# Query tiles of one attention unit with two buffers, in place of tiles of two units with one buffer

## The chip, the cores and the metric

The kernel runs on one core of a Trainium2 chip. A core has five engines with a queue of instructions each: TensorE (PE, matrix products), VectorE (DVE), ScalarE (ACT), GpSimd (POOL) and SyncE (SP, which here only starts transfers). An engine takes its instructions in the order of its queue; an instruction that waits for another engine or for a transfer holds everything behind it. Transfers are started from the queues of SP and ACT. The metric is the time on the device in microseconds (us), from one launch to its end.

## What is computed

Attention with a top-32 mask over 4 batches, 8 heads, 576 positions and 64 channels, followed by two feed-forward layers of 512 to 2048 to 512 over the 2304 tokens, the first with a rational function, the second with h*cos(h):

```python
scores = scale * np.matmul(q, k.transpose(0, 1, 3, 2))
kth = np.partition(scores, -top_k, axis=-1)[..., -top_k:-top_k + 1]
mask = scores >= kth
scores = np.where(mask, scores, -1000000000.0)
scores = scores - np.max(scores, axis=-1, keepdims=True)
attn = np.exp(scores)
attn = attn / (np.sum(attn, axis=-1, keepdims=True) + 1e-09)
return np.matmul(attn, v).astype(np.float32)
...
h = x @ w_in
g = P / (Q + 1e-06)          # P, Q: polynomials of h and |h|
x = g @ w_out
...
h = x @ w_in
g = h * np.cos(h)
return (g @ w_out).astype(np.float32)
```

All is float32. To keep that precision the kernel splits most operands of its matrix products into a rounded high part (type float32r) and the rest (low part), and adds two or three products.

## The kernel before

**Units and pieces.** Attention is cut into 72 units. A unit is 128 query rows of one pair of heads. Eight units (4 pairs of heads times 2 row tiles) make one block of 256 tokens; there are 9 blocks. Two neighbouring units, an even one and the odd one behind it, share the pair of heads and the block, so their queries lie side by side in memory. The program is written as a list of pieces, five for each unit (p = 0 to 4). In a piece of unit i stand steps of several units: the scores of unit i+1 (`qk`, L328), the top-32 search of unit i (`topk`, L356), the end of the mask and the product with V of unit i-1 (`av`, L405), and steps of the feed-forward layers of earlier blocks (`in1`, `pol1`, `end1`, `low1`, `out1` and their likes of the second layer).

**Scores.** `qk(i)` makes the scores of the two heads j = 0 and 1 in turn. For each it runs four matmuls into one PSUM tile `sx`: high part of q times k (L346) and low part of q times k (L348), for two halves of the keys. ACT then copies `sx` to `sS`. For units 0 to 7 (the first block) the raw q is used without a split (L343). The first half of `qk(i+1)` stands at the head of unit i, the second in its piece p = 0 (for units 20 and up).

**Queries.** `load_q(i)` (L194) fetches the tile `qr`, 128 partitions x 2 x 256 values, 256 KB, the queries of units i and i+1, by a transfer that is started from ACT's queue. It stands in p = 1 of an even unit, two units ahead. `split_q(i)` (L200) has ACT copy `qr` with rounding into `qh` and, one piece later, has DVE (for i from 20 to 71) or POOL (before) subtract `qh` from `qr` into `ql`. It stands in p = 3 and p = 4 of an even unit and serves the two units that follow. `qr`, `qh` and `ql` have one buffer each (`QRB`, `QHB` = 1): a new `qh` can be written only when the last matmul that reads the old one is done, and that is the second half of `qk(i+1)`, where i is the even unit in which the split stands.

**Order.** The order within each queue is made when the kernel is built, by a planned timeline that starts whatever is ready, the earlier written first. Three wrappers add to that. `InOrder` (L91) holds DVE, in units 20 to 71, to the order in which the program is written. `Behind` (L114) makes POOL's instructions there wait for the last instruction of DVE other than MAX8 and MATCH_REPLACE8 that was written before them. `Windowed` (L72) bounds how far an engine may run ahead in the first pieces. In units 20 to 71 the order on DVE is therefore: in p = 0 the feed-forward steps `end1` (u, q, u, u), the mask of the unit before (e), max and min of two halves of the scores (e), `mid2` (rr); then rounds of MAX8 and MATCH_REPLACE8 up to p = 4; then, in even units, the subtraction into `ql`.

**Phases.** Units 0 to 19, up to about 340 us, run beside the conversion of the weights. Units 20 to 71 end at about 1160 us. Behind them stand only feed-forward steps.

Of the kernel before, what the change touches and what calls it, by code (L numbers as in the profile page):

```python
# [23 lines left out]
P = 128  # L24
# [10 lines left out]
BT = 2 * P  # L35
# [22 lines left out]
DGL, E1P, M2P, LAL = 0, 4, (12, 12), 3  # L58
DV1, DV2 = 8, 7
KB, VB, XB = 2, 2, 2  # L60
SQ, OBB, EB = 3, 1, 2
QRB, QHB = 1, 1
LQ = 1
S0, MD, O1P, I2, O2, SB = 46, 4, 1, 2, 3, 4
U0, U1 = 20, 72
C0, C1 = 5 * U0, 5 * U1 - 4
# [64 lines left out]
def body(tc, out, qt, kt, vt, ident_d, w1_d, w1o_d, a_d, b_d, w2_d, w2o_d):  # L131
    nc = tc.nc
    V, A = InOrder(tc, nc.vector, WIN, C0), Windowed(tc, nc.scalar, WA, PA)
    G = Behind(tc, nc.gpsimd, WG, PG, v=V)
    PE, SP = nc.tensor, nc.sync

    with ExitStack() as ctx:
# [6 lines left out]
        att = pool("att", 2)  # L144
# [20 lines left out]
        nu = len(units)  # L165
# [23 lines left out]
            SP.dma_start(out=x[:, 0].bitcast(F32), in_=kt[b, pr])  # L189
            return x  # L190

        qpair, vlast = {}, [None]
# [42 lines left out]

        load_q(0)
        load_k(0)
        ident = cst.tile([P, P], F32)
        SP.dma_start(out=ident, in_=ident_d)
        nident = cst.tile([P, P], F32R)  # L240
# [86 lines left out]

        def qk(i):  # L328
            n, pr = units[i]
            raw, hi, lo = (*qpair[i // 2], None, None)[:3]  # L330
            kvs = ins[i]
            m = P // len(kvs)
            st[i] = sb = att.tile([P, 2, S], F32, tag="sS", bufs=2, name=f"sS{i}")
            for j in range(2):
                rows = slice(j * D, (j + 1) * D)
                for c, (k, _) in reversed(list(enumerate(kvs))):
                    q0 = i % 2 * P
                    qs, qc = slice(0, (c + 1) * m), slice(q0, q0 + (c + 1) * m)
                    for hf in range(2):
                        o = sx[qs, hf, :HALF]  # L340
                        hs = slice(hf * HALF, (hf + 1) * HALF)
                        if n < 2:
                            mm = PE.matmul(o, raw[rows, j, qc], k[rows, 0, hs].bitcast(F32), start=True, stop=True)  # L343
                            after(mm, hf)
                        else:
                            mm = PE.matmul(o, hi[:, j, qc], k[:, j, hs], start=True, stop=False, skip_group_check=True)  # L346
                            after(mm, hf)
                            mm = PE.matmul(o, lo[:, j, qc], k[:, j, hs], start=False, stop=True, skip_group_check=True)  # L348
# [379 lines left out]
        def attention():  # L728
            load_k(1)
            load_v(0)  # L730
            for _ in qk(0):
                pass
            prev = None
            nrm, fresh, held, sq = [], [], [], None
            for i in range(nu + 1):
                if LQ == 0 and i % 2 == 0 and i + 2 < nu:
# [12 lines left out]
                for p in range(5):  # L749
                    if p == 0 and grouped:  # L750
                        yield
                        next(prev)
                        next(prev)
                        next(t)
                    elif p == 0:
                        if prev is not None:
                            next(prev)
                        next(t, None)
                        if prev is not None:
                            next(prev)  # L760
                        next(t, None)
                    else:
                        next(t, None)
                    if p == 0:
                        if prev is not None:
                            a = av(i - 1)
                            next(a)
                        next(nq, None)
                        if prev is not None:
                            next(a, None)  # L770
                            if i % 4 == 0:
                                nrm.append(norm((i - 1) // 8, (i - 1) // 4 % 2))
                                next(nrm[-1])
                                next(nrm[-1])
                                fresh.append(nrm[-1])
                        if 0 < i < nu:
                            load_v(i)
                    if p == LQ > 0 and i % 2 == 0 and i + 2 < nu:
                        load_q(i + 2)
                    if p == SQ and i % 2 == 0 and 8 <= i + 2 < nu:  # L780
                        sq = split_q(i + 2)
                        next(sq, None)
                    if p == SQ + 1 and sq is not None:
                        next(sq, None)
                        sq = None
                    if fresh and p == (4 if grouped else 1):
                        next(fresh.pop())
                    if len(nrm) == 2 and (p == 4 or p == 1 and not grouped):
                        for x in nrm if grouped else nrm[:1] if p == 1 else nrm[1:]:
                            next(x, None)  # L790
                        if p == 4:
                            nrm = []
                    yield
                prev = t
# [61 lines left out]
```

## Time and profile before

| | |
|---|---|
| median of 3 runs | 1379.81 us (1376.72 to 1381.07) |
| the profiled execution, time | 1384.74 us |
| the profiled execution, span from the first to the last instruction | 1383.0 us |
| mean granted TensorE clock, share of full speed | 0.940 |

Most numbers below come from the one profiled execution, which took 4.93 us more than the median. Of its 1384.74 us, 1383.0 us are the span and 1.74 us lie around it. In the rows, a name such as `ql<-qr,qh` gives what an instruction writes and what it reads. Most helper calls are recorded under one line, L81, so the tile names are what tells them apart. A bracket at the end of a line gives how long the engine stood idle before it, and what ended that.

### The profile page before, as it was taken

Reading aid. Unit: us, or ns where it says so; the run is one execution under the profiler, and the core shown is the slowest. Engines: PE = TensorE matmul, PEld = TensorE weight load, DVE = VectorE, ACT = ScalarE, POOL = GpSimd, SP = SyncE. Lnnn points to the kernel's source line nnn. Section 1 sums busy time; section 2 is a strip of 40 time slices with the busy share of each in tenths; the row PEclk is TensorE's granted clock in tenths of the full one; section 3 lists DMA queues with packets and bytes.
Section 4 is the critical chain, followed back from the end, with each engine's and each line's share of the span. In section 5 each row is a group of like instructions: output and inputs, shape, how many; then the busy total and the mean of one; then the engine's idle time right before and its main releaser. Section 6 shows DMA issues by size and latency. Waiting matters only on the chain.

```text
span 1383.0 us, 24902 instructions
## 1 busy us (share of the span) xinstructions
PE 1234.3 (89%) x8944; PEld 1100.5 (80%) x8944; DVE 1184.1 (86%) x2477; ACT 1082.2 (78%) x1886; POOL 599.3 (43%) x439
## 2 busy tenths in 40 slices
PE   5676678666998999999999999999999999999997
PEld 2344566555888999899899989998999989899986
DVE  6989987889999998989999998999898888666533
ACT  6876777775787888888888888888888778697653
POOL 2666445543245554535564363545353534430000
PEclk9856788777999999999999999999999999999999
DMA  7996767693557756666776755665666778567787
GB/s 236 331 308 203 241 190 221 235 320 122 160 178 245 255 196 219 199 218 213 240 252 235 236 199 195 210 215 188 218 210 230 265 257 277 194 214 249 237 273 227
DMA packets 141547, 314.97 MB, mean 228 GB/s; under 512 B 12016, under 2 KB 28528, under 8 KB 141424
## 3 DMA queue, kind: packets, MB, share of 16 engines
q1 hardware_dynamic: 122832, 261.99, 57.3%
q10 hardware_dynamic: 18592, 51.39, 11.0%
q8 instruction: 71, 1.16, 0.3%
q14 instruction: 52, 0.43, 0.1%
HBM read 278.20 MB, written 35.13 MB: 227 GB/s over the span
## 4 chain that ended last, share of the span: by engine, by line
PE 47%; DVE 23%; ACT 12%; DMA 10%; issue 4%; POOL 3%; SPq 0%; ACTq 0%; POOLq 0%; DVEq 0%
DVE e L81 10%; PE o L639 8%; PE h L499 6%; PE h L501 6%; PE h L500 6%; DVE hd L81 4%; DVE u L81 4%; PE y L570 3%; PE y L571 3%; PE sx L439 3%; PE y L569 3%; PE sx L346 2%; DMA w2o<-w2o 2%; ACT r L81 1%; PE sx L348 1%
## 5 line engine op out<-in xcount | busy, mean ns | idle before, releaser
L81 DVE MAX8 hd<-e 128x8 f32<-128x288 f32 (+1 forms) x576 | 320.6, 595 | 0.0
L81 DVE MATCH_REPLACE8 e<-hd,e 128x288 f32<-128x288 f32 (+1 forms) x432 | 230.6, 540 | 0.0
L639 PE MATMUL o<-w2o,gg 128*128 128x512 f32 x864 | 218.0, 396 | 3.1 <-DMA w2o<-w2o 2.5
L639 PEld LDWEIGHTS o<-w2o,gg 128*128 128x128 f32 x864 | 155.6, 189 | 37.7 <-DMA w2o<-w2o 3.8
L570 PE MATMUL y<-gg,w1o 128*128 128x256 f32 x576 | 169.0, 293 | 8.5 <-POOL gg L81 8.5
L499 PE MATMUL h<-xh,w1hi 128*128 128x256 f32 x576 | 170.9, 297 | 5.9 <-ACT pt24a L81 1.6
L569 PE MATMUL y<-gg,w1o 128*128 128x256 f32 x576 | 171.0, 297 | 2.9 <-ACT gg L81 2.9
L81 POOL TENSOR_TENSOR rr<-rr,hs 128x512 f32<-128x512 f32 x56 | 72.7, 1300 | 222.5 <-DVE rr L81 127.2
L571 PE MATMUL y<-gg,w1ol 128*128 128x256 f32 x576 | 167.2, 290 | 1.2 <-DMA w1ol<-w1ol 1.2
L500 PE MATMUL h<-xl,w1hi 128*128 128x256 f32 x576 | 167.1, 290 | 0.0
L501 PE MATMUL h<-xh,lo 128*128 128x256 f32 x576 | 166.4, 289 | 0.5 <-DMA lo<-w1lo 0.5
L501 PE MATMUL h<-x2h,lo 128*128 128x256 f32 x576 | 163.5, 284 | 0.7 <-DMA lo<-w2lo 0.6
L499 PE MATMUL h<-x2h,w2hi 128*128 128x256 f32 x576 | 163.8, 285 | 0.2 <-ACT pt64b L81 0.2
L500 PE MATMUL h<-x2l,w2hi 128*128 128x256 f32 x576 | 163.3, 284 | 0.0
L81 POOL TENSOR_TENSOR gg<-u,gg 128x512 fp32r<-128x512 f32 x64 | 85.2, 1332 | 139.0 <-DVE rr L81 86.8
L81 DVE TENSOR_TENSOR e<-sS 128x576 f32<-128x576 f32 x144 | 125.5, 911 | 16.1 <-PE sx L425 8.8
L81 DVE SCALAR_TENSOR_TENSOR e<-sS,hd,e 128x576 f32<-128x576 f32 x144 | 130.7, 935 | 4.7 <-ACT e L81 4.6
L81 POOL TENSOR_TENSOR cb<-cb,raw 128x512 int32<-128x512 int32 x64 | 91.6, 1433 | 81.6 <-DVE cb L81 73.1
L570 PEld LDWEIGHTS y<-gg,w1o 128*128 128x128 f32 x576 | 114.4, 199 | 12.0 <-POOL gg L81 10.0
L499 PEld LDWEIGHTS h<-xh,w1hi 128*128 128x128 f32 x576 | 114.0, 198 | 10.6 <-ACT pt24a L81 1.8
L569 PEld LDWEIGHTS y<-gg,w1o 128*128 128x128 f32 x576 | 114.1, 198 | 5.7 <-ACT gg L81 3.7
L571 PEld LDWEIGHTS y<-gg,w1ol 128*128 128x128 f32 x576 | 114.3, 198 | 2.6 <-DMA w1ol<-w1ol 1.4
(1028 smaller groups left out, 3656.4 us busy)
## 6 DMA issues: line engine op xcount, KB each, us to landing
w2o<-w2o SPq DMA_DIRECT2D x144, 512.0 KB, 4.4
lo<-w1lo SPq DMA_DIRECT2D x72, 512.0 KB, 3.9
w1ol<-w1ol SPq DMA_DIRECT2D x72, 512.0 KB, 4.3
lo<-w2lo SPq DMA_DIRECT2D x72, 512.0 KB, 4.8
k<-kdr ACTq DMA_DIRECT2D x44, 576.0 KB, 4.8
raw<-w SPq DMA_DIRECT2D x32, 512.0 KB, 5.3
v<-vt ACTq DMA_DIRECT2D x48, 320.0 KB, 5.2
qr<-qt ACTq DMA_DIRECT2D x36, 256.0 KB, 3.8
```

Source lines behind the costliest of these rows:

```text
L81: r = f(*a, **k)
L346: mm = PE.matmul(o, hi[:, j, qc], k[:, j, hs], start=True, stop=False, skip_group_check=True)
L348: mm = PE.matmul(o, lo[:, j, qc], k[:, j, hs], start=False, stop=True, skip_group_check=True)
L439: mm = PE.matmul(o, v[:, kc * P + j * D:kc * P + (j + 1) * D], pj[j][:, kc, qs], start=False, stop=(kc == 3), skip_group_check=True)
L499: PE.matmul(h[:, i, :], wh, xh[:, c, :], start=(c == 0), stop=False)
L500: PE.matmul(h[:, i, :], wh, xl[:, c, :], start=False, stop=False)
L501: PE.matmul(h[:, i, :], lo[:, i, c, :], xh[:, c, :], start=False, stop=(c == NCC - 1))
L569: PE.matmul(y[:, c, :], w1o[:, f, cs], gh[:, i, :], start=(f == 0 and c % 2 == 0), stop=False, skip_group_check=True)
L570: PE.matmul(y[:, c, :], w1o[:, f, cs], gl[:, i, :], start=False, stop=False, skip_group_check=True)
L571: PE.matmul(y[:, c, :], wl[:, i, cs], gh[:, i, :], start=False, stop=(f == NF - 1), skip_group_check=True)
L639: PE.matmul(o[:, t, :], l[:, i, ts], wt[i][:, r], start=(f == 0 and r == 0 and l is gh), stop=(f == NF - 1 and l is gl), skip_group_check= ...
```

## The change

A tile of q now holds one unit: 128 partitions x 2 x 128 values, 128 KB. The raw tile `qr` has two buffers. High and low part lie in one tile `q` of 2 x 2 x 128 values, with two buffers. So 6 KB for each partition hold queries before and after. Each unit has its own fetch, copy and subtraction. In unit i, p = 0 subtracts for unit i+2 (`low_q`; on DVE in units 20 to 71, on POOL before), p = 1 fetches for unit i+4 (for i+3 while the first block runs), and p = 2 copies for unit i+3 (`high_q`). The subtraction stands at the end of what attention does in p = 0, so on DVE it lies between max and min of the scores and `mid2`.

```diff
+QRB, QB = 2, 2
...
         def load_q(i):
-            k, pr = units[i][0] // 2, units[i][1]
-            raw = att.tile([P, 2, BT], F32, tag="qr", bufs=QRB, name=f"qr{i}")
-            A.dma_start(out=raw, in_=qt[k, pr])
-            qpair[i // 2] = (raw,)
-
-        def split_q(i):
-            raw, = qpair[i // 2]
-            hi = att.tile([P, 2, BT], F32R, tag="qh", bufs=QHB, name=f"qh{i}")
-            lo = att.tile([P, 2, BT], F32R, tag="ql", bufs=QHB, name=f"ql{i}")
-            A.activation(hi, raw, AF.Copy)
-            qpair[i // 2] = (raw, hi, lo)
-            if U0 <= i < U1:
-                yield
-                V.tensor_sub(lo, raw, hi.bitcast(F32))
-            else:
-                G.tensor_sub(lo, raw, hi.bitcast(F32))
+            if i < nu:
+                k, pr = units[i][0] // 2, units[i][1]
+                raw = att.tile([P, 2, P], F32, tag="qr", bufs=QRB, name=f"qr{i}")
+                A.dma_start(out=raw, in_=qt[k, pr, :, :, i % 2 * P:(i % 2 + 1) * P])
+                qs_[i] = [raw, None]
+
+        def high_q(i):
+            if 8 <= i < nu:
+                qs_[i][1] = x = att.tile([P, 2, 2, P], F32R, tag="q", bufs=QB, name=f"q{i}")
+                A.activation(x[:, 0], qs_[i][0], AF.Copy)
+
+        def low_q(i, E):
+            if 8 <= i < nu:
+                raw, x = qs_[i]
+                E.tensor_sub(x[:, 1], raw, x[:, 0].bitcast(F32))
...
-                    if p == LQ > 0 and i % 2 == 0 and i + 2 < nu:
-                        load_q(i + 2)
-                    if p == SQ and i % 2 == 0 and 8 <= i + 2 < nu:
-                        sq = split_q(i + 2)
-                        next(sq, None)
-                    if p == SQ + 1 and sq is not None:
-                        next(sq, None)
-                        sq = None
+                    if p == 0:
+                        low_q(i + 2, V if grouped else G)
+                    if p == 1:
+                        if i + 1 < 8:
+                            load_q(i + 3)
+                        if i + 2 >= 8:
+                            load_q(i + 4)
+                    if p == 2:
+                        high_q(i + 3)
```

`grouped` is true in units 20 to 71. The matmuls of `qk` keep their number, shapes and order; they read the unit's own tile.

## Rows read from the trace of the kernel before

**Rows 1.** The page's first part: busy time, share of the span and instructions.
```profile
PE 1234.3 (89%) x8944; PEld 1100.5 (80%) x8944; DVE 1184.1 (86%) x2477; ACT 1082.2 (78%) x1886; POOL 599.3 (43%) x439
```
**Rows 2.** Windows: length, busy PE, PEld, DVE, ACT, POOL (instructions), clock, DMA share, GB/s.
```profile
773.50:900.00 126.50, 122.60 (x963) 115.03 (x962) 117.40 (x259) 107.28 (x187) 59.20 (x45) 0.99 0.63 209
900.00:1026.50 126.50, 122.61 (x962) 115.01 (x962) 117.38 (x259) 107.23 (x187) 59.17 (x45) 0.99 0.63 210
```
**Rows 3.** Waits of DVE, 773.5 to 900 us: us in total, times, longest us.
```profile
DVE ql L81 <- ACT qh L81: 5.8, 2, 3.4
DVE rr L81 <- ACT n L81: 2.4, 1, 2.4
DVE q L81 <- ACT r L81: 0.5, 1, 0.5
```
**Rows 4.** Timeline, 784 to 794 us: start, us, engine, line, operation, tiles, shapes.
```profile
786.12 1.44 ACT L81 ACTIVATE e<-sS,nb 128x576 f32<-128x576 f32 x2
...
786.46 0.29 PE L348 MATMUL sx<-k,ql 128*128 128x288 f32 x1
...
787.45 0.62 ACT L81 ACTIVATE qh<-qr 128x512 fp32r<-128x512 f32 x1
...
788.11 0.69 DVE L81 TENSOR_TENSOR ql<-qr,qh 128x512 fp32r<-128x512 f32 x1 [2.35 <-ACT qh L81]
...
788.72 0.74 DVE L81 SCALAR_TENSOR_TENSOR u<-u,nega,w 128x512 f32<-128x512 f32 x1
788.83 0.34 ACTq L81 DMA_DIRECT2D qr<-qt  x1
...
792.85 1.42 DVE L81 TENSOR_TENSOR e<-sS 128x576 f32<-128x576 f32 x2
```
**Rows 5.** Waits of DVE, then of ACT, 300 to 1100 us.
```profile
DVE ql L81 <- ACT qh L81: 29.6, 12, 3.4
...
ACT qh L81 <- PE sx L346: 8.1, 12, 1.6
```
**Rows 6.** The chain that ended last, 500 to 950 us: start, us, work.
```profile
535.87 0.63 ACT qh L81
...
913.91 0.63 ACT qh L81
```
**Rows 7.** Waits of PE, 773.5 to 900 us.
```profile
PE y L570 <- POOL gg L81: 1.8, 1, 1.8
```
**Rows 8.** Windows behind that wait (columns as in rows 2).
```profile
828.00:833.00 5.00, 5.00 (x30) 5.00 (x31) 5.00 (x14) 4.45 (x9) 4.01 (x4) 0.66 0.02 7
```
**Rows 9.** Groups by line and shape, whole run: busy us, mean ns | idle before.
```profile
L81 DVE MAX8 hd<-e 128x8 f32<-128x576 f32 x288 | 203.7, 745 | 0.0
...
L81 DVE MAX8 hd<-e 128x8 f32<-128x288 f32 x288 | 117.0, 445 | 0.0
...
L81 ACT ACTIVATE qh<-qr 128x512 fp32r<-128x512 f32 x32 | 20.0, 625 | 8.5 <-PE sx L346 8.4
...
L81 DVE TENSOR_TENSOR ql<-qr,qh 128x512 fp32r<-128x512 f32 x26 | 17.8, 684 | 39.5 <-ACT qh L81 39.5
...
L81 POOL TENSOR_TENSOR ql<-qr,qh 128x512 fp32r<-128x512 f32 x6 | 9.3, 1549 | 15.4 <-ACT qh L81 10.5 <-DMA w2o<-ch 4.9
```
**Rows 10.** Timeline of DVE, 816 to 818 us.
```profile
816.59 0.67 DVE L81 TENSOR_TENSOR ql<-qr,qh 128x512 fp32r<-128x512 f32 x1
817.18 0.74 DVE L81 SCALAR_TENSOR_TENSOR u<-u,nega,w 128x512 f32<-128x512 f32 x1
```
**Rows 11.** Instructions on tile qr: its fetch (ns min/median/max), and time to landing.
```profile
L81 ACTq DMA_DIRECT2D qr<-qt x36: 334/335/468, 0.7 to 1107.3; - x36
...
DMA to landing us min/median/max: 2.4/3.8/6.9
```
**Rows 12.** A window behind the last unit (columns as in rows 2).
```profile
1200.00:1250.00 50.00, 49.69 (x401) 47.94 (x402) 26.15 (x35) 37.34 (x57) 15.50 (x12) 1.00 0.61 204
```

More of the change, by code (lines that the diff above doesn't have):

```diff
@@ L60 @@
 KB, VB, XB = 2, 2, 2
-SQ, OBB, EB = 3, 1, 2
-QRB, QHB = 1, 1
-LQ = 1
+OBB, EB = 1, 2
+QRB, QB = 2, 2
 S0, MD, O1P, I2, O2, SB = 46, 4, 1, 2, 3, 4
@@ L190, in prep @@
             return x
-        qpair, vlast = {}, [None]
+        qs_, vlast = {}, [None]
         def load_q(i):
-            k, pr = units[i][0] // 2, units[i][1]
-            raw = att.tile([P, 2, BT], F32, tag="qr", bufs=QRB, name=f"qr{i}")
-            A.dma_start(out=raw, in_=qt[k, pr])
-            qpair[i // 2] = (raw,)
-        def split_q(i):
-            raw, = qpair[i // 2]
-            hi = att.tile([P, 2, BT], F32R, tag="qh", bufs=QHB, name=f"qh{i}")
-            lo = att.tile([P, 2, BT], F32R, tag="ql", bufs=QHB, name=f"ql{i}")
-            A.activation(hi, raw, AF.Copy)
-            qpair[i // 2] = (raw, hi, lo)
-            if U0 <= i < U1:
-                yield
-                V.tensor_sub(lo, raw, hi.bitcast(F32))
-            else:
-                G.tensor_sub(lo, raw, hi.bitcast(F32))
+            if i < nu:
[11 more added lines that the diff above has]
+                E.tensor_sub(x[:, 1], raw, x[:, 0].bitcast(F32))
         def load_k(i):
@@ L237, in body @@
         load_k(0)
+        load_q(1)
         ident = cst.tile([P, P], F32)
@@ L329, in qk @@
             n, pr = units[i]
-            raw, hi, lo = (*qpair[i // 2], None, None)[:3]
+            raw, x = qs_.pop(i)
+            hi, lo = (x[:, 0], x[:, 1]) if x is not None else (None, None)
             kvs = ins[i]
@@ L336, in qk @@
                 for c, (k, _) in reversed(list(enumerate(kvs))):
-                    q0 = i % 2 * P
-                    qs, qc = slice(0, (c + 1) * m), slice(q0, q0 + (c + 1) * m)
+                    qs = slice(0, (c + 1) * m)
                     for hf in range(2):
@@ L342, in qk @@
                         if n < 2:
-                            mm = PE.matmul(o, raw[rows, j, qc], k[rows, 0, hs].bitcast(F32), start=True, stop=True)
+                            mm = PE.matmul(o, raw[rows, j, qs], k[rows, 0, hs].bitcast(F32), start=True, stop=True)
                             after(mm, hf)
                         else:
-                            mm = PE.matmul(o, hi[:, j, qc], k[:, j, hs], start=True, stop=False, skip_group_check=True)
+                            mm = PE.matmul(o, hi[:, j, qs], k[:, j, hs], start=True, stop=False, skip_group_check=True)
                             after(mm, hf)
-                            mm = PE.matmul(o, lo[:, j, qc], k[:, j, hs], start=False, stop=True, skip_group_check=True)
+                            mm = PE.matmul(o, lo[:, j, qs], k[:, j, hs], start=False, stop=True, skip_group_check=True)
                         order[hf] = [mm.ins.name]
@@ L732, in attention @@
                 pass
+            load_q(2)
             prev = None
-            nrm, fresh, held, sq = [], [], [], None
+            nrm, fresh, held = [], [], []
             for i in range(nu + 1):
-                if LQ == 0 and i % 2 == 0 and i + 2 < nu:
-                    load_q(i + 2)
                 nq = qk(i + 1) if i + 1 < nu else iter(())
@@ L777, in attention @@
                             load_v(i)
-                    if p == LQ > 0 and i % 2 == 0 and i + 2 < nu:
-                        load_q(i + 2)
-                    if p == SQ and i % 2 == 0 and 8 <= i + 2 < nu:
-                        sq = split_q(i + 2)
-                        next(sq, None)
-                    if p == SQ + 1 and sq is not None:
-                        next(sq, None)
-                        sq = None
+                    if p == 0:
[7 more added lines that the diff above has]
+                        high_q(i + 3)
                     if fresh and p == (4 if grouped else 1):
```

## The prediction

> **What bounds the kernel now.** I read the busy shares first, then windows of eight units, then who waits for whom, then the chain of work that ended last, and at last the timeline around the one step that the change moves. By the busy shares of the whole run PE leads with 89%, DVE follows with 86% and ACT with 78% [rows 1]. That is an average over three phases, so it decides nothing yet.
>
> Units 20 to 71 repeat every eight units, in about 126.5 us, and two such stretches look alike to within 0.1 us [rows 2]. In the first of them PE is busy 122.60 us, so it idles 3.9; DVE is busy 117.40 and idles 9.1; ACT idles 19.2, which is 2.4 us for each unit. Of DVE's 9.1 us, 5.8 + 2.4 + 0.5 = 8.7 are three waits [rows 3]. DVE takes its instructions in the written order here, so a wait holds all that stands behind it: DVE is working or held in 126.1 of 126.5 us, which makes it the tightest engine, with PE close behind. Its largest wait is the one for `qh`, twice in a stretch.
>
> The timeline shows how that wait comes about [rows 4]. DVE stands 2.35 us before the subtraction into `ql`, until 788.11. It waits for ACT's rounding copy into `qh`, which runs from 787.45. The copy could not start earlier than about 786.7, for the last matmul that reads the old `qh` and `ql` starts at 786.46 and takes 0.29 us, and there is one buffer; by then ACT was in two exponentials (786.12, 1.44 us). Behind the subtraction DVE has the feed-forward steps u, q, u, u, on which POOL and then PE wait.
>
> Between 300 and 1100 us this wait comes 12 times and costs DVE 29.6 us; the copy itself waits for matmuls 12 times, 8.1 us in all [rows 5]. In the chain that ended last the copy stands four times between 500 and 950 us, once for each stretch; the first and the last are shown [rows 6]; the other wait of a stretch is not on it.
>
> Behind the last unit PE is busy 49.69 of 50 us and DVE 26.15 [rows 12]: there nothing that is done to q can shorten anything.
>
> **The change part by part.**
>
> *The copy.* It moves from p = 3 of the unit before its use by two pieces and a unit ahead. With two buffers of one unit it writes over unit i+1 while it stands in unit i, so it still waits for the second half of `qk(i+1)`, the same matmuls as before. What changes is the deadline. Before, DVE wanted the result one piece later; now it wants it in p = 0 of the next unit, behind u, q, u, u, the two masks and max and min. In the timeline the matmul ends near 786.75, and max and min of the next p = 0 end at 794.27 [rows 4]; without the wait and the subtraction ahead of them that would be near 791.3, so ACT has about 4.5 us in which to place a copy of half a microsecond. I take the wait for `qh` as gone: 29.6 us less in DVE's queue at most.
>
> *ACT's work.* 32 copies of 512 values become 64 of 256. A whole copy takes 625 ns [rows 9]; a half one lies between 313 ns and that, so the addition is between 0 and 32 x 0.625 = 20 us over the run. I take 5 us, from the slope of DVE's MAX8 below, as the nearest pair of shapes. It is covered by ACT's idle 2.4 us per unit, of which 5 us over 64 units use 0.08. Without that cover it would cost the 5 us. The copy's own wait for matmuls can come twice as often, which is 16 us in place of 8.1, or 0.2 us a unit, and lies in the same cover.
>
> *DVE's work.* 26 subtractions of 512 values become 50 of 256 (units 22 to 71; units 20 and 21 go to POOL). MAX8 takes 745 ns for 576 values and 445 for 288 [rows 9], so 1.04 ns a value; a half subtraction is then 684 - 267 = 417 ns, and the pair costs 0.15 us more than the whole. In the queue the next instruction starts 0.59 us after the subtraction's start [rows 10], so a half one may take up only 0.32 us and the pair 0.06 us more. Added: 25 x 0.06 to 25 x 0.15 = 1.5 to 3.8 us. I take the upper end, since a result is awaited at its end.
> [...]
>
> *POOL's work.* Before unit 20, 6 subtractions of 1549 ns [rows 9] become 14 halves. A half takes between 0.77 and 1.55 us, so 14 take 10.8 to 21.7 in place of 9.3. POOL is busy 43% [rows 1] and I take nothing for it, with 12 us as the worst, all of it exposed. The two waits named in the same row, 15.4 us, may go with the longer lead, so the other end is as far below nothing.
>
> *Transfers.* 36 fetches become 72, each of half the bytes but in runs of 512 bytes in place of 2 KB. A fetch of 256 KB lands in 3.8 us, at most 6.9 [rows 11]; the new ones are asked for more than a unit, 15.8 us, before the copy. Even at twice the longest they are hidden. Starting one takes 0.335 us in ACT's queue [rows 11], so 36 more are 12 us at most, or 0.25 us a unit, in ACT's cover; in the timeline ACT's engine ran on beside it.
>
> *A wait that is added.* The fetch for unit i+4 goes into the buffer that the subtraction for unit i+2 has just read, and stands one piece behind it. ACT's queue is held until DVE is done with it. Behind it stand the copies of transposed scores, `sS` and the exponentials, on which PE and DVE wait. Such a hold is there already: the fetch was started at 788.83, 0.03 us after the subtraction ended (788.11 + 0.69) [rows 4], and ACT lost next to nothing. It will come in each unit in place of every second. I take nothing for it, as in that row, and price the other end as a rival.
>
> *What is late next.* Without the wait DVE reaches u, q, u, u 2.35 us sooner, so POOL's subtraction `gg` comes sooner too, on which PE stood 1.8 us in this stretch [rows 7]. [...] Then ACT is next: DVE's wait for `n` (2.4 us) and for `r` [rows 3] will grow a little, for ACT is paced by PE's results.
>
> **The sum.** On the chain the wait stands four times: 4 x 2.35 = 9.4 us. The loss of clock goes in the two stretches that show 0.99 [rows 2]: 2 x 1.7 = 3.4. Against that, the chain carries the subtraction in eight places or so: 8 x 0.15 = 1.2. Gain 9.4 + 3.4 - 1.2 = 11.6 us. The profiled execution would go from 1384.7 to 1373.1; it lay 4.9 us above the median of 1379.8, which goes to **1368**. The bounds of the unknown costs (POOL 12 us more, or 15 us less) put this case between 1352 and 1380, the likeliest part being 1360 to 1375.
>
> **The rivals.**
>
> *The whole wait comes out.* All 29.6 us of DVE's wait turn into time, less 1.5 of added work: 28.1, so 1352. For it: DVE is working or held nearly always. Against it: PE has only 3.9 us of idle time in 126.5, and 29.6 us over 6.3 stretches are 4.7 each.
>
> *PE binds and nothing is gained.* If PE's 122.6 us and the waits on ACT that have nothing to do with q set the pace, DVE only waits elsewhere, and the time stays at 1379, between 1376 and 1384. The chain speaks against it, since it runs through DVE from 788 us on.
> [...]
>
> *The wait stays.* ACT's copy still waits for the same matmuls. If the queue's order places it late, DVE waits in p = 0 instead and only the costs are left: 1379.8 + 3.8 = 1384.
>
> *ACT is held by the fetch: slower.* If ACT comes to the fetch when DVE has only begun p = 0, it is held until the subtraction is done, by the timeline about 5.5 us (788.72 to 794.27 [rows 4]), and the exponentials and `sS` of that unit come late. ACT can lose 2.4 us a unit before it sets the pace; from there on each hold counts. Once in eight units, as the order repeats: (5.5 - 2.4) x 6.5 = 20 us, so 1400; once in sixteen, 1390. For it: every unit now has such a fetch, and ACT has long waits on PE and POOL of its own. Against it: the plan places the fetch where the subtraction should be done, and the one hold seen cost nothing.
>
> **How the numbers follow.** Forecast 0.45 (1368); the whole wait 0.12 (1352); PE binds 0.14 (1379); the wait stays 0.07 (1384); ACT held 0.22 (1390 to 1400). The order of every queue is planned anew, which can move the first 340 us either way; that is in the POOL bounds. The range leaves out about one in ten at each end: the lower part of the whole wait, and the dearer half of the held fetch: 1348 to 1392. A measurement of this kernel tells about 0.3% from no change, 1375.7 to 1384.0. Faster takes the forecast and the whole wait, 0.57. Same takes PE binding and most of the staying wait, 0.20. Slower takes the held fetch and the rest, 0.23.
>
> **What would show it.** Right: DVE's wait for the copy below 5 us in all, between 300 and 1100 us; stretches of eight units of about 124.5 us; no mean clock of 0.99 in them; ACT's idle time before instructions that follow a fetch as now. Wrong: a wait of DVE for ACT's copy in p = 0; fetches that start right behind the subtraction with ACT idle for over a microsecond before them; or DVE waiting for `n`, `r` or the exponentials by as much as it had waited for `qh`.

## The result: slower by 0.9%, and what the profile shows

The changed kernel takes 1391.56 us (median of 4 runs, 1390.32 to 1395.74) against 1380.44 beside it: 1.0091 times the time before, with an interval of 1.0063 to 1.0120. The forecast was 1368, so even the sign is wrong; the time lies at the foot of the rival "ACT is held by the fetch". The profiled execution took 1395.74 us, 1393.9 of them span.

The busy shares of the page hardly differ from [rows 1]:
```profile
PE 1245.6 (89%) x8944; PEld 1104.1 (79%) x8944; DVE 1172.3 (84%) x2501; ACT 1084.9 (78%) x1918; POOL 584.2 (42%) x447
```
Where the time went shows in the timeline of DVE, at max and min of the scores of unit 20 and of unit 71 (two of these instructions a unit, so units can be counted). Before:
```profile
366.74 1.42 DVE L81 TENSOR_TENSOR e<-sS 128x576 f32<-128x576 f32 x2
...
1181.94 1.43 DVE L81 TENSOR_TENSOR e<-sS 128x576 f32<-128x576 f32 x2 [0.38 <-ACT sS L81]
```
After:
```profile
350.21 1.42 DVE L80 TENSOR_TENSOR e<-sS 128x576 f32<-128x576 f32 x2
...
1193.96 1.43 DVE L80 TENSOR_TENSOR e<-sS 128x576 f32<-128x576 f32 x2 [0.57 <-ACT sS L80]
```
So the whole is a sum of two large changes of opposite sign: the first 20 units end 16.5 us sooner, and units 20 to 71, where the gain was forecast, take 843.8 us in place of 815.2, 28.6 more. The rest behind unit 71 is 1 us shorter. (The section on the kernel before puts the ends of its phases at about 340 and 1160 us; by this count they lie at 367 and 1182.)

DVE's waits between 300 and 1100 us, to be read beside [rows 5] and [rows 3] (total, times, longest):
```profile
DVE e L80 <- ACT sS L80: 42.2, 21, 3.8
DVE q L80 <- ACT r L80: 13.4, 10, 2.2
DVE rr L80 <- ACT n L80: 11.4, 12, 2.2
```
The wait for the rounding copy, 29.6 us before, is gone, as the prediction said. In its place DVE waits 42.2 us for the scores `sS`. The window of one repeat of the schedule (eight units, columns as in [rows 2]) is 128.0 us long in place of 126.5:
```profile
770.90:898.90 128.00, 122.10 (x960) 113.38 (x960) 116.42 (x262) 107.12 (x192) 57.38 (x44) 1.00 0.63 204
```
PE's 122 us of work are the same as in [rows 2]; its idle time went from 3.9 to 5.9 us. This repeat is a mild one. From max to max, units 48 to 55 take 1.5 us more than before, units 40 to 47 take 6.6 more, and from the max of unit 64 to that of unit 71 it is 11.7. The windows of the whole stretch, before and then after:
```profile
366.74:1181.94 815.20, 787.49 (x6250) 736.62 (x6251) 758.37 (x1647) 684.83 (x1191) 392.11 (x289) 0.99 0.67 223
```
```profile
350.21:1193.96 843.75, 798.04 (x6251) 740.56 (x6250) 751.35 (x1673) 687.78 (x1215) 377.41 (x289) 0.99 0.66 215
```
PE idles 45.7 us in place of 27.7, and the same number of matmuls keeps it busy 10.6 us longer. Part of that is the clock. In windows of half a microsecond over these two stretches it reads 1.00 or 0.50, and a value between only where it changes. With a wait of PE of 2.54 us, up to 1104.70, it falls from 1.00 to 0.50:
```profile
1105.00:1110.00 5.00, 5.00 (x24) 4.93 (x24) 4.78 (x10) 0.65 (x1) 3.17 (x3) 0.50 0.39 146
```
PE's busy time in these half microseconds, times the share of the clock that is missing, gives an estimate of what the low clock cost: 5.1 us before and 10.6 after, so about 5.5 us of the longer busy time.

The timeline from 784 to 801 us shows one repeat from near by:
```profile
784.87 0.30 PE L347 MATMUL sx<-k,q 128*128 128x288 f32 x1
...
785.20 0.65 ACT L80 ACTIVATE sS<-sx 128x576 f32<-128x576 f32 x1
...
785.75 0.41 ACT L80 ACTIVATE q<-qr 128x256 fp32r<-128x256 f32 x1
...
785.89 1.43 DVE L80 TENSOR_TENSOR e<-sS 128x576 f32<-128x576 f32 x2 [1.20 <-ACT sS L80]
...
787.23 0.42 DVE L80 TENSOR_TENSOR q<-qr,q 128x256 fp32r<-128x256 f32 x1
...
787.68 0.56 ACTq L80 DMA_DIRECT2D qr<-qt  x1
...
787.83 0.27 PE L438 MATMUL sx<-pt45b,v 128*64 128x128 f32 x1
...
788.29 0.28 ACT L80 ACTIVATE xs<-sx 128x128 f32<-128x128 f32 x1 [2.13 <-DVE rr L80]
...
788.62 0.40 PE L345 MATMUL sx<-k,q 128*128 128x288 f32 x1 [0.52 <-ACT xs L80]
...
794.99 0.27 PE L424 MATMUL sx<-ident,e 128*128 128x128 f32 x1
...
800.60 0.29 PE L345 MATMUL sx<-k,q 128*128 128x288 f32 x1
```
Two things are to be seen. The fetch of the next q starts 0.03 us after DVE's subtraction (787.23 + 0.42), for it goes into the buffer that the subtraction has read, and ACT's engine stands 2.13 us until the copy `xs` behind it. That is not all the fetch's doing: `xs` copies the product with V, whose last matmul ends at 788.10 (787.83 + 0.27), so the fetch, whose start lasts to 788.24, put `xs` off by no more than 0.2 us here. And the scores are late: they are in `sS` at 785.85, and DVE, which has stood 1.20 us for them, begins at 785.89. Worked out from the trace, as a mean over units 24 to 67, the second `sS` of a unit is ready 5.2 us ahead of its max and min before, and 1.4 us after.

The lateness comes from the order of PE's queue. In the changed kernel the last of the nine transposes of `e` starts 9.1 us behind this max (794.99), and the second half of the next scores, which follows it in the same PSUM tile `sx`, 14.7 us behind it (800.60). Before, with max at 792.85 [rows 4], these are 4.0 and 7.7 us:
```profile
796.86 0.27 PE L425 MATMUL sx<-ident,e 128*128 128x128 f32 x1
...
800.56 0.30 PE L346 MATMUL sx<-k,qh 128*128 128x288 f32 x1
```

On the tile `qr` the changed kernel shows its parts (ns min/median/max) and the time to landing, beside [rows 9] and [rows 11]:
```profile
L80 ACTq DMA_DIRECT2D qr<-qt x72: 547/553/662, 0.7 to 1120.0; - x72
...
L80 ACT ACTIVATE q<-qr x64: 401/410/432, 105.1 to 1154.4; 128x256 fp32r<-128x256 f32 x64
L80 DVE TENSOR_TENSOR q<-qr,q x50: 371/418/423, 351.9 to 1155.9; 128x256 fp32r<-128x256 f32 x50
L80 POOL TENSOR_TENSOR q<-qr,q x14: 727/734/1252, 106.4 to 330.6; 128x256 fp32r<-128x256 f32 x14
...
DMA to landing us min/median/max: 2.3/4.2/7.9
```

### The profile page after: what moved, and what is told of

It reads as the page before. It is cut to its first block, busy times and chain, and to the rows that moved or that the text cites. A ratio compares the mean times of both kernels' runs of the same rounds, so it can differ in the third digit from the quotient of the medians.

```text
span 1393.9 us, 25000 instructions
## 1 busy us (share of the span) xinstructions
PE 1245.6 (89%) x8944; PEld 1104.1 (79%) x8944; DVE 1172.3 (84%) x2501; ACT 1084.9 (78%) x1918; POOL 584.2 (42%) x447
## 3 DMA queue, kind: packets, MB, share of 16 engines
q10 hardware_dynamic: 32992, 51.39, 11.4%
## 4 chain that ended last, share of the span: by engine, by line
PE 50%; ACT 19%; DVE 13%; DMA 11%; issue 3%; POOL 3%; ACTq 0%; SPq 0%; POOLq 0%; DVEq 0%
PE o L638 9%; PE h L498 7%; PE h L499 7%; PE h L500 7%; DVE e L80 6%; DVE hd L80 3%; PE y L570 3%; PE y L569 3%; PE sx L438 3%; PE y L568 3%; ACT L80 2%; DMA k<-kdr 2%; ACT r L80 2%; PE sx L345 2%; ACT sS L80 2%
## 5 line engine op out<-in xcount | busy, mean ns | idle before, releaser
L498 PE MATMUL h<-xh,w1hi 128*128 128x256 f32 x576 | 172.9, 300 | 10.3 <-ACT xh L80 0.8
L80 DVE TENSOR_TENSOR e<-sS 128x576 f32<-128x576 f32 x144 | 121.8, 885 | 61.1 <-ACT sS L80 55.1
L499 PE MATMUL h<-xl,w1hi 128*128 128x256 f32 x576 | 170.3, 296 | 2.0 <-POOL xl L80 1.5
L80 DVE SCALAR_TENSOR_TENSOR e<-sS,hd,e 128x576 f32<-128x576 f32 x144 | 123.1, 880 | 12.3 <-ACT e L80 12.1
L80 ACT ACTIVATE sS<-sx 128x576 f32<-128x576 f32 x144 | 92.9, 645 | 40.4 <-PE sx L347 31.7
L499 PEld LDWEIGHTS h<-xl,w1hi 128*128 128x128 f32 x576 | 116.2, 202 | 4.5 <-POOL xl L80 3.2
L569 PEld LDWEIGHTS y<-gg,w1o 128*128 128x128 f32 x576 | 113.0, 196 | 7.3 <-POOL gg L80 6.1
## 6 DMA issues: line engine op xcount, KB each, us to landing
qr<-qt ACTq DMA_DIRECT2D x72, 128.0 KB, 4.2
```

The lines of the kernel that those rows point to most:

```text
L80: r = f(*a, **k)
L498: PE.matmul(h[:, i, :], wh, xh[:, c, :], start=(c == 0), stop=False)
L499: PE.matmul(h[:, i, :], wh, xl[:, c, :], start=False, stop=False)
L569: PE.matmul(y[:, c, :], w1o[:, f, cs], gl[:, i, :], start=False, stop=False, skip_group_check=True)
```

## The experiments

Three theories stood at the start. **Held fetch**: ACT's queue stands for DVE's subtraction, and that makes the rest late. **Order**: the queues' new plan puts the scores late. **Lost wait**, the prediction's own: DVE's wait for the copy was time, so a loss must come from new work. One table holds all runs. "Unit 20" is the start of its max and min, "20 to 71" the time from there to that of unit 71, "DVE waits most for" its largest wait between 340 and 1150 us, all from each kernel's one profiled execution. "Second scores" is how far behind the max of a unit the second half of the next unit's scores starts on PE (mean over units 24 to 67). The ratio is given as its 95% interval, against runs of the kernel before beside it. In a wait `DVE q <- ACT q` of these kernels q is the query tile, in `DVE q <- ACT r` the feed-forward step of that name.

| kernel | median us | ratio to before | unit 20 | 20 to 71 | second scores | DVE waits most for |
|---|---|---|---|---|---|---|
| before | 1380 | | 366.7 | 815.2 | 8.1 | copy of q, 39.5 |
| after | 1391.56 | 1.0063 to 1.0120 | 350.2 | 843.8 | 13.1 | sS, 43.4 |
| late | 1381.94 | 0.9985 to 1.0024 | 347.5 | 833.2 | 13.1 | sS, 61.2 |
| runs1k | 1406.05 | 1.0139 to 1.0223 | 365.4 | 837.4 | 13.4 | sS, 59.5 |
| sub4 | 1381.17 | 0.9978 to 1.0019 | 351.4 | 828.5 | 6.9 | copy of q, 62.7 |
| noq_b | 1397.13 | 1.0064 to 1.0148 | 361.8 | 829.0 | 13.4 | sS, 69.8 |
| late_sc | 1369.18 | 0.9896 to 0.9930 | 349.3 | 818.8 | 9.2 | transposes, 32.1 |
| paired | 1368.23 | 0.9870 to 0.9941 | 348.6 | 822.1 | 8.1 | copy of q, 33.9 |
| lq2 | 1376.23 | 0.9946 to 0.9981 | 362.1 | 813.3 | 8.0 | copy of q, 38.5 |
| b_sc | 1386.65 | 1.0026 to 1.0054 | 366.4 | 818.3 | 8.7 | copy of q, 37.8 |
| paired_all | 1374.21 | 0.9927 to 0.9966 | 352.3 | 819.3 | 8.0 | copy of q, 32.8 |
| late_md | 1370.46 | 0.9898 to 0.9952 | 347.9 | 818.6 | 9.2 | transposes, 35.5 |
| noq_sc | 1404.87 | 1.0144 to 1.0206 | 362.9 | 837.0 | 10.3 | transposes, 84.0 |
| late_p2 | 1376.15 | 0.9954 to 0.9995 | 352.4 | 823.1 | 9.0 | transposes, 31.5 |

The column of the second scores parts the kernels. In before, lq2, paired, paired_all and sub4 the last transpose starts 3.0 to 4.2 us behind max, the second scores 6.9 to 8.1 and the product with V 11.4 to 12.5. In after, late, runs1k and noq_b these are 8.8 to 9.3, 13.1 to 13.4 and 16.7 to 17.0, which is in the next unit, ahead of that unit's scores. In the first five DVE has a subtraction of q ahead of the feed-forward steps; in the other four it has none there, and noq_b has none at all. The first five take 813.3 to 828.5 us for units 20 to 71, the other four 829.0 to 843.8. In b_sc, late_sc, late_md, late_p2 and noq_sc the place of the scores was set by the edit.

**late: the fetch put behind a late step of the unit, so that it holds ACT less.**
```diff
-                A.dma_start(out=raw, in_=qt[k, pr, :, :, i % 2 * P:(i % 2 + 1) * P])
+                r = A.dma_start(out=raw, in_=qt[k, pr, :, :, i % 2 * P:(i % 2 + 1) * P])
+                if nbs.get(i - 4):
+                    tc.add_manual_dep(r.ins, nbs[i - 4], ORDER, reason="late fetch")
...
-                        if i + 2 >= 8:
+                        if i + 2 >= 8 and not grouped:
                             load_q(i + 4)
+                    if p == 4 and grouped:
+                        load_q(i + 4)
```


> The changed kernel, but in units 20 to 71 the fetch stands behind the unit's small ACT step nb, late in the unit, by which time the subtraction that it waits for is long done. Held fetch (ACT's queue stands for DVE's subtraction, so the copies sS come late): ACT's idle time around the fetches between 340 and 1150 us falls from 23.8 us to under 6, DVE's wait for sS falls from 42 us to under 20, the stretch of eight units from 127.9 to 126 us or less, the time from 1391.6 to 1378 or less. Order (the planned order puts the score copies late, whatever the fetch does): the idle time goes but DVE's wait for sS stays above 35 us and the time within 1386 to 1396.

ACT's idle time right around the fetches from 340 to 1150 us (end of the instruction before to start of the one behind) is 3.9 us before, 23.8 after and 2.7 here. Not all of the 23.8 us is the hold: eleven of the 13 gaps of over 1 us end within 0.2 us of the PE work that ACT's next instruction reads. Counted from the end of what the next instruction reads, an estimated 7 us are left. Units 20 to 71 get 10.6 us shorter and the time falls by 9.6, back to that of before, while the order on PE stays late (13.1 us). So the place of the fetch is worth about 10 us, some 0.2 us a unit, of which the trace shows an estimated 7.

PE's wait for the fetches of `k`, 300 to 1160 us, falls with it, in the changed kernel and in late:
```profile
PE sx L345 <- DMA k<-kdr: 10.5, 4, 4.7
```
```profile
PE sx L347 <- DMA k<-kdr: 0.7, 1, 0.7
```
These fetches are started from ACT's queue too, but a fetch of q is not what delays them. Each of the four that PE waits for in the changed kernel starts within 0.2 us of the end of the last score matmul that reads the old `k`; the longest wait:
```profile
1058.70 0.85 ACTq L80 DMA_DIRECT2D k<-kdr  x2
...
1058.90 0.29 PE L347 MATMUL sx<-k,q 128*64 128x288 f32 x1
...
1066.82 0.58 PE L345 MATMUL sx<-k,q 128*128 128x288 f32 x1 [4.68 <-DMA k<-kdr]
```
From unit 64 on each unit reads two `k`, and there are two buffers, so late scores make the next `k` late. DVE's wait for `sS` did not fall in late, it grew to 61.2 us: the other 18 us over before are not the hold. Neither expectation came out whole, and the time lies between the two.

**runs1k: each unit's 1 KB in one run, by the layout of q in memory.**
```diff
-                A.dma_start(out=raw, in_=qt[k, pr, :, :, i % 2 * P:(i % 2 + 1) * P])
+                A.dma_start(out=raw, in_=qt[k, pr, i % 2])
...
+    qt = qt.reshape(NB, NP, P, 2, 2, P).transpose(0, 1, 4, 2, 3, 5)
```


> The changed kernel with q laid out so that a unit's 1 KB per partition is one run in place of two of 512 bytes; everything else is the same. Long start (a fetch of 512-byte runs takes 0.55 us to start in ACT's queue against 0.335 before): the start falls to about 0.34 us, 0.21 us x 48 = 10 us of ACT's time in units 20 to 71, and the time falls by 3 to 10 us, to 1382 to 1388. Held fetch or order: the start falls as well, but ACT still stands until the subtraction is done, and the time stays within 1388 to 1395.

The fetch takes what it took before to start:
```profile
L80 ACTq DMA_DIRECT2D qr<-qt x72: 334/335/1037, 0.7 to 1130.1; - x72
```
Units 20 to 71 are 6.4 us shorter than after, within what the long start would give. But the first 20 units lost all they had gained, 15 us, with the same steps in the program, so the time is the worst of all, outside both expectations. No theory had that in its numbers, and what the start costs is not settled by this run.

**sub4: the subtraction back ahead of the feed-forward steps.**
```diff
-                    if p == 0:
+                    if p == 0 and i <= U0:
                         low_q(i + 2, V if grouped else G)
+                    if p == 4 and grouped:
+                        low_q(i + 3, V)
```


> The changed kernel, but in units 20 to 71 the subtraction stands in p = 4 of the unit before, ahead of the feed-forward steps, where the kernel before has it, and not between max and min and mid2. Place (the subtraction in p = 0 delays mid2 and what POOL does behind it): DVE's waits for r and n, 18.4 and 11.4 us, fall to near the 1.8 and 8.9 of before, and the time to 1380 to 1386. Held fetch: the fetch is released some 5 us sooner, so ACT is held less and DVE's wait for sS falls by half, the time to 1380 or less. Order: no change of either, 1386 to 1396. The copy may now come late again, which would show as a wait of DVE for it of 20 us or more and a time above 1390.

The wait for the copy comes back, 62.7 us against 39.5 before, and yet units 20 to 71 are 15 us shorter than in the changed kernel, and the time is that of before:
```profile
DVE q L80 <- ACT q L80: 62.7, 26, 4.6
```
The expectation that tied this wait to a slow kernel missed. A wait of DVE for the copy of 62.7 us goes with a shorter stretch than a wait for `sS` of 43.4. What was expected of the place came out: the waits for `r` and `n` fell to 1.3 and 6.1 us, and the time lies in its range. But the edit does more than one thing. ACT's idle time around the fetches falls to 2.0 us, and PE's order is the early one again, so the run does not tell their shares apart.

**noq_b: no work on q at all from unit 20 on, in the kernel before.**
```diff
                     if p == LQ > 0 and i % 2 == 0 and i + 2 < nu:
-                        load_q(i + 2)
+                        if i + 2 < U0:
+                            load_q(i + 2)
+                        else:
+                            qpair[i // 2 + 1] = qpair[i // 2]
-                    if p == SQ and i % 2 == 0 and 8 <= i + 2 < nu:
+                    if p == SQ and i % 2 == 0 and 8 <= i + 2 < U0:
```


> The kernel before, with fetch, copy and subtraction of q left out for units 20 and up (their scores are made from the last tile before, so they are not the reference's). It bounds what any arrangement of these steps can gain there. If DVE's wait for the copy was real time, as the prediction had it, units 20 to 71 become 12 to 30 us shorter than before (817 us from the first max of unit 20 to the last of 71) and the time is 1350 to 1368. If other engines set the pace and the wait cost next to nothing, these units keep 812 us or more and the time is 1374 to 1382.

Fewer instructions, no copy to wait for, and units 20 to 71 take 829.0 us, 13.8 more than before. DVE's time went into the same wait as in the changed kernel:
```profile
DVE e L81 <- ACT sS L81: 69.8, 29, 4.8
```
With the wait and all its work removed nothing is gained, which speaks against the lost wait. It does not refute it by itself, for PE's queue has the late order here (13.4 us): what the wait is worth with everything else as before no run shows. The time missed both expectations.

**late_sc and late_md: the scores earlier in PE's queue, on top of late.** In late_sc both halves of the next scores stand at the head of the unit; in late_md the second half stands in p = 0, ahead of the transposes.
```diff
-                if not U0 <= i < U1:
-                    next(nq, None)
+                next(nq, None)
```
```diff
                     if p == 0:
+                        if grouped:
+                            next(nq, None)
                         if prev is not None:
                             a = av(i - 1)
                             next(a)
```


> The run late (fetch behind nb), and in units 20 to 71 both halves of the next unit's scores stand at the head of the unit, where the second half stood in p = 0 behind the transposes. In late DVE waits 61 us for sS between 340 and 1150 us. Score order (the place of the scores in PE's queue now sets DVE's pace): sS ends 5 us or more ahead of max and min in place of 1.3, DVE's wait for sS falls under 20 us, units 20 to 71 shrink from 833 us to 815 or less and the time from 1382 to 1358 to 1366. PE binds (DVE only waits for whichever comes last): the wait for sS falls but another takes its place, units 20 to 71 stay at 825 to 840 us and the time at 1376 to 1390.

> The run late, with the second half of the next unit's scores in p = 0 ahead of the transposes of the unit before, in place of behind them (late_sc has it at the head of the unit). Score order: what counts is that it is ahead of the transposes, so DVE's wait for sS falls from 61 us to under 20, units 20 to 71 take 815 to 822 us as in late_sc (819) and the time is 1364 to 1374. If only the place at the head helps, they stay at 828 to 836 us and the time at 1378 to 1386.

Both go the way of the score order: 818.8 and 818.6 us against 833.2, and 1369 and 1370 us. late_md lies in the range expected of it; late_sc had been expected at 815 us and 1366 at most. `sS` is ready 4.0 us ahead of max and min in both, against 1.3 in late, and the wait for it is gone from the list of late_sc:
```profile
DVE e L80 <- PE sx L427: 32.1, 21, 5.8
DVE q L80 <- ACT r L80: 17.6, 18, 1.8
DVE e L80 <- ACT e L80: 11.3, 20, 1.1
```
DVE still waits, for transposes that read the buffer `e`, for `r` and for the exponentials, but PE idles less, 19 us in place of 27 of the 500. The windows from 600 to 1100 us of late and of late_sc:
```profile
600.00:1100.00 500.00, 472.97 (x3717) 440.78 (x3715) 453.91 (x1014) 411.58 (x729) 226.41 (x175) 0.99 0.63 215
```
```profile
600.00:1100.00 500.00, 480.75 (x3812) 446.62 (x3808) 453.31 (x1019) 419.42 (x742) 229.32 (x175) 1.00 0.67 223
```
**b_sc** is late_sc's edit on the kernel before, as a control.

> The kernel before with both halves of the next unit's scores at the head of the unit in units 20 to 71, as in late_sc. Score order: before has 5.2 us between the end of sS and max and min, so more lead gains nothing; the time stays within 1374 to 1388. If it becomes much slower, above 1390, scores that come early cost on their own (they push other work on PE back), and late_sc carries that cost too.

It is 0.4% slower, 3 us of it in units 20 to 71. As a control it says little: the second scores start no sooner than before (8.7 us against 8.1), and `sS` is 4.5 us ahead of max in place of 5.2, so the scores did not gain lead here.

**paired and paired_all: tiles of one unit, at the times of the kernel before.** In paired this holds from unit 20 on; in paired_all in the first 20 too (there with POOL in p = 3).
```diff
+                    elif i % 2 == 0:
+                        for j in (i + 2, i + 3):
+                            if p == 1 and j > U0 + 3:
+                                load_q(j)
+                            if p == 3 and j > U0 + 2:
+                                high_q(j)
+                            if p == 4:
+                                low_q(j, V)
```


> The changed kernel's tiles of one unit throughout, but from unit 20 on two units are fetched, copied and subtracted together at the places of the kernel before (p = 1, 3 and 4 of an even unit), so that DVE waits for the copy again. Pace (the units gained nothing from the earlier copy and lost to the holds and the late scores): DVE's wait for the copy comes back with 25 to 45 us, its wait for sS falls under 10, units 20 to 71 go from 844 us back to 812 to 822, and with the first 20 units as short as in the changed kernel (first max of unit 20 at 350 us) the time is 1360 to 1372. Prediction's view (the wait is lost time): units 20 to 71 become longer than in the changed kernel and the time is above 1391.

> As the run paired, but in the first 20 units too the steps of two units stand together at the places of the kernel before; only the tiles are one unit wide. It asks why units 0 to 19 end 15 to 19 us sooner in the changed kernel (first max of unit 20 at 350 us against 367). Lead (the copy and POOL's subtraction come a unit sooner, so POOL, which waited 15 us for them in the kernel before, no longer holds the conversion of the weights): the gain goes, unit 20 starts at 360 to 370 us and the time is 1378 to 1388. Size (half tiles, freed one by one, let fetches and copies start sooner): the gain stays, unit 20 starts at 346 to 354 us and the time is 1362 to 1374. A start outside both would leave it to the plan of the queues, which moved unit 20 by 5 us in lq2 and noq_b with no such cause.

In paired DVE's wait for the copy returns and the stretch falls to 822 us, the upper edge of what was expected; the time is 1368, with late_sc the best. Its largest wait, and its window from 600 to 1100 us:
```profile
DVE q L80 <- ACT q L80: 33.9, 13, 4.9
```
```profile
600.00:1100.00 500.00, 483.50 (x3755) 451.17 (x3755) 463.45 (x1017) 418.67 (x740) 235.22 (x175) 0.98 0.65 219
```
PE idles 16.5 of these 500 us, against 27.0 in late. PE's order is the early one again (8.1 us), and ACT idles 3.4 us around the fetches. So it is the early place of the steps on q that cost time in units 20 to 71, not the width of the tiles; fetch, copy and subtraction were moved back together here. paired_all keeps the gain of the first 20 units (352.3 us), so it is not the lead of the copy that gave it. POOL's waits for the copy, 0 to 350 us, agree: in the changed kernel and in paired_all they are
```profile
POOL q L80 <- ACT q L80: 25.1, 8, 8.1
```
```profile
POOL q L80 <- ACT q L80: 3.6, 2, 2.5
```
and the first 20 units are as short with either.

**lq2 and late_p2: a fetch with time to spare, written one piece later.** lq2 is the kernel before with `LQ` = 2; late_p2 is late_md with the fetch of the first 20 units in p = 2.
```diff
-LQ = 1
+LQ = 2
```
```diff
-                    if p == 1:
+                    if p == 2 and not grouped:
                         if i + 1 < 8:
```


> The kernel before with the fetch written one piece later, which has 14 us to spare. Nothing that any engine waits for changes, only the plan of the queues is made anew. If replanning alone moves little, the time is that of before within 0.3%, 1376 to 1385. If it moves as much as the changes tried here, the time lies 5 to 20 us away, either way, mostly in the first 20 units.

> The run late_md with the fetch of the first 20 units written one piece later, which has a unit to spare. It asks whether the gain in the first 20 units (unit 20 at 348 us against 367 in the kernel before) belongs to the half tiles or to one lucky plan of the queues; runs1k, with the same tiles and 1 KB runs, had lost it (365 us). Half tiles: unit 20 starts at 344 to 354 us, and the time is 1364 to 1376. Plan: it starts anywhere between 350 and 368 us, as likely above 358, and units 20 to 71, whose program is that of late_md, keep 815 to 822 us; above 358 the time is 1376 to 1388.

They measure the plan alone. lq2 moves the first 20 units by 4.6 us and the rest by 2; late_p2 keeps the gain of the first 20 (352.4) but moves units 20 to 71, whose steps are those of late_md, by 4.5 us. Differences of 5 us in a stretch are therefore no evidence, and 10 us is no safe bound either: runs1k moved the first 20 units by 15 us with the same steps, and noq_b and noq_sc, which only leave work out, made units 20 to 71 longer by 14 and 22. The verdicts above rest on the order and the waits in the traces as much as on the times.

**noq_sc: noq_b with both halves of the scores at the head.**

> The run noq_b (no fetch, copy or subtraction of q from unit 20 on, scores of later units made from an old tile and so not the reference's) with both halves of the scores at the head of the unit. It bounds what the best arrangement of the q steps could give beside early scores. If the q steps cost time of their own in late_sc (819 us for units 20 to 71), these units take 800 to 812 us here. If PE and its order set the pace, they take 813 to 825 us, and 829 as in noq_b was all score order.

It misses on every side: 837.0 us, longer than noq_b, and DVE waits for the transposes:
```profile
DVE e L81 <- PE sx L425: 84.0, 30, 5.6
```
The second scores come at 10.3 us in place of noq_b's 13.4. So early scores are no cure in themselves; they helped where the rest of the order suited them.

## Why the prediction was wrong

**What held.** The wait for the copy vanished, from ACT's queue to DVE's. A half subtraction takes 418 ns on DVE, against 417 worked out from MAX8. A half copy takes 410 ns on ACT, within its bounds; the 64 copies cost 6.2 us more than the 32, against the 5 taken. POOL's halves take 734 ns, a little below the lower bound of 0.77. The landing (4.2 us, at most 7.9) stayed hidden for q itself.

**The step that failed first is what bounds the kernel.** DVE was "working or held in 126.1 of 126.5 us", and from this followed that its waits are time: the sum counts the wait for the copy four times, 9.4 us. But an engine that takes its work in order shows its slack as waits (in noq_b, with less work, DVE waits 69.8 us for `sS`), so DVE held nearly always does not tell who sets the pace. In the changed kernel the wait for the copy is gone, DVE waits 42.2 us for the scores in its place, and units 20 to 71 are 28.6 us longer. No kernel without that wait has a shorter stretch than before, and the shortest of all, lq2, keeps it (38.5 us). The four places in the chain [rows 6] did not show a price either: the chain says what came last in that run, not what comes last when it is gone. So neither the 9.4 us nor the rival's 28 came in any run; what the wait would be worth with PE's order unchanged stays open. Nor does any run show the 3.4 us that the sum takes for the clock: the spell of low clock in [rows 8] cost an estimated 1.7 us (5 x 0.34), but units 20 to 71 of the changed kernel have six such spells in place of three, an estimated 10.6 us in place of 5.1. PE, busy in 97% of the stretch, idles 25 to 33 us in the kernels that take up to 823 us for it and 41 to 49 in those that take 829 or more (sub4, with 828.5, has 31). That by itself does not prove that PE sets the pace, for with equal work every engine idles more in a longer stretch. The rival "PE binds" had no gain, with 0.14, and no loss.

**The step that was put at nothing is the order of the queues.** The prediction let the new plan move the first 340 us alone. In units 20 to 71 it moved PE's queue too: the second scores start 13.1 us behind max in place of 8.1. Of the 28.6 us, 18.0 are left when the fetch is put late (late), and 14.4 of these go when the scores are moved up in PE's queue (late_sc, late_md agree to 0.2 us). The last 3.6 are within what a new plan moves. sub4, paired and paired_all put the subtraction back and have the early order again; noq_b, which has no subtraction, has the late one. So the order goes with the subtraction ahead of the feed-forward steps, and with DVE's wait for the copy that comes with it. Why the plan does that is not shown.

**The step that mis-sized a term is the wait that is added.** I took nothing for the hold of ACT, since one row showed that it cost nothing, and held that ACT could lose 2.4 us a unit. Measured, ACT stands 23.8 us around 48 fetches, 0.5 us each, of which an estimated 7 us are the hold, and putting the fetch late gives 10.6 us. That is far below 2.4 us a unit, so ACT's idle time was no cover. A likely reason, argued and not shown, is that PE waits for single results of ACT's, such as `xs`, in between. The rival had the hold and its place right, but not the order; its price (5.5 us once in eight units) and its point of decision were wrong. That the time came out near its 1390 is luck: 10.6 us for the fetch and 18.0 for the order, less 16.5 in the first 20 units.

One reading was wrong without harm: the copy moves by one piece and a unit for the first unit of a pair, and by one piece for the second, not by two pieces and a unit.

**The first 20 units** were taken at nothing, between 15 us less and 12 more, for POOL. They gave 16.5 us. The reason that I had for a gain, the longer lead, is not it (paired_all). Eight kernels with half tiles have the gain, though most share the program of these units and only paired_all and late_p2 differ in it; runs1k, with half tiles and other runs in memory, has not. Whether it is the size or the plan stays open.

A kernel that beats both came out of it: half tiles at the old times (paired, 1368.23 us, 0.9905 of before) or at the new times with late fetches and earlier scores (late_sc, 1369.18, 0.9913).

## What to carry to other kernels

A wait on an engine that runs in order need not be a price: here no kernel without the wait for the copy had a shorter stretch than the 815.2 us of before. Before counting such a wait, leave the awaited work out of a kernel altogether and see whether the stretch gets shorter, and whether the other queues kept their order; here it got longer (829.0 us, noq_b), and they had not. The fetch, which reuses a buffer, waited in the queue of ACT, which starts it, and started 0.03 us after the subtraction that reads the buffer; so ask which engine such a transfer holds and what stands behind it, and where there is slack, start it a little later, when its buffer is free for certain (late, 9.6 us less than the changed kernel). Where the order of queues is planned by a program, measure first how far a change with no effect of its own moves the time, and look at each stretch by itself, since a gain and a loss can hide each other.

## What the runs showed of the hardware that was not expected

The time to start a transfer on ACT's queue did not go with its bytes: 0.335 us for 256 KB in 128 runs of 2 KB [rows 11], 0.335 us for 128 KB in 128 runs of 1 KB (runs1k), and 0.553 us for 128 KB in 256 runs of 512 bytes. Whether it is the number of runs or their size that counts, these three shapes do not tell apart. The prediction had taken 0.335 for each of the new ones, so starts cost 72 x 0.553 = 40 us of ACT's queue over the run where 24 were expected.
